# First halves one step sooner, and weight conversions dealt out: a fused gated-attention and SoLU kernel on Trainium2

## The chip, the cores and the metric

The kernel runs on one core of one Trainium2 chip. The metric is the device time of one execution in microseconds (us). Below, PE is TensorE, DVE is VectorE, ACT is ScalarE, POOL is GpSimd and SP is the engine whose queue issues most of the transfers.

## What is computed

Two blocks follow each other. The first is a gated linear attention over 4 batches, 8 heads, 768 tokens and a head size of 48, the second a feed-forward block over the 3072 tokens, with 384 inputs, 1024 hidden units and a layer norm between its two products. The reference, cut to its core:

```python
for t in range(S):
    state = alpha[:, :, t, :, None] * state + np.einsum('bhd,bhe->bhde', k[:, :, t], v[:, :, t])
    y[:, :, t] = np.einsum('bhd,bhde->bhe', q[:, :, t], state)
...
x = np.ascontiguousarray(attn_out.transpose(0, 2, 1, 3)).reshape(B * S, H * D)
...
h = x @ w_in
e = np.exp(h - h_max)
sm = e / (np.sum(e, axis=-1, keepdims=True) + 1e-09)
solu = h * sm
ln = (solu - mu) / np.sqrt(var + 1e-06) * g_ln
return (ln @ w_out).astype(np.float32)
```

The weights `w_in` and `w_out` arrive as 64-bit floats and are turned into 32-bit floats by integer and float operations on DVE.

## The kernel before

The 768 tokens are cut into 6 groups of 128. A group holds 4 batches, so the feed-forward works on 6 times 512 tokens, and its output on 24 chunks of 128 tokens, numbered n = 4 g + b. Period g is the time in which group g goes through the first product of the feed-forward, in 8 steps s (one for each 128 of the 1024 hidden units). In the same steps the attention of group g + 1 and the second product of group g - 1 are done. All of the order is written out by hand: each engine runs its instructions in the order of the program.

**A step.** `up(g, s)` is six PE instructions for h (`up_mm`; a product of 32-bit floats is two instructions in the trace), then ACT's exponential e, DVE's product u = h e and ACT's square of u (`up_act`). The banks for h are two, so the up of step s waits for the product of step s - 2. `running(g, s)` adds up e (on POOL) and the squares (on DVE) over the steps into p; in the last group DVE sums u too. At the next period's start `token_sums` takes p's sums over partitions (PE matmuls into `rows`, DVE's transpose into `cols`).

**The downs.** `down(n, half)` is the second product of chunk n for four of the eight hidden blocks: eight PE instructions into one of two banks `o`. The list `todo` holds the eight halves of one group, and each step of the next period takes one off its front. Behind a second half, the next step's up is followed by `finish(n)`: three small DVE instructions, a power on POOL (`r`), a scaled copy on ACT (`o_sb`), and an output transfer on SP. The last group's eight halves stand behind the last period, with its `token_sums` and `last_norm` behind the first of them.

**The attention.** The names in the tables `usual` and `first` place the parts of the next group's attention at the head of a step, behind the up, in the middle or at the tail: transposes and scans on DVE, `queries` and `keys` on POOL, `apart` and the copies of `keys_back` on ACT, `scores`, `read_state`, `read_values` and `next_state` on PE. `read_values` ends with four ACT copies that make the next group's x.

**Period 0.** It comes first and holds, beside group 0's ups, the conversion of the weights in 8 pieces: pieces 0 to 3 are `w_in`, 4 to 7 `w_out`. `fetch` brings the raw bits into one of six slots of `room`, `in_range` is two ACT instructions (and two short reads of an accumulator) that test a piece, `bits` is the conversion by five DVE instructions (L612, L615, L620, L623, L624), and `scaled` is the multiplication of two rows of blocks of `w_out` by the gain on ACT. Behind the loop over f stand, in this order, `bits(6)`, the transposes of k, the second `array_sums`, `down(0, 0)`, `bits(7)`, `token_sums(0)`, `alpha_T(1)`, `down(1, 0)`, the scans of group 1, and `mean`, which takes the mean of the weights over the hidden units (`mean(0)` is L645). Then come group 1's queries and scores (L278).

Of the kernel before, what the change touches and what calls it, by code (L numbers as in the profile page):

```python
# [11 lines left out]
U32 = mybir.dt.uint32  # L12
I32 = mybir.dt.int32
AF = mybir.ActivationFunctionType
ALU = mybir.AluOpType
# [17 lines left out]
def fast_path(ctx, tc, q, k, v, alpha, moe_w_in, moe_w_out, moe_g_ln, out):  # L33
# [13 lines left out]
    B, H, S, D = q.shape  # L47
    NTOK, DM = out.shape
    DFF = moe_w_in.shape[1]
    G = S // P  # L50
# [5 lines left out]
    FC = DFF // P  # L56
# [116 lines left out]
    def load_v(g):  # L173
        t = slice(g * P, (g + 1) * P)
        for b in range(B):
            nc.sync.dma_start(out=held(vn, b), in_=v[b, :, t, :].rearrange("h p d -> p h d"))
# [188 lines left out]
    def next_state(g):  # L365
        kv = banks("kv", [H, D], 2)
        for h in range(H):
            for c in range(2):
                for r in range(4):
                    b = 2 * (r // 2) + c  # L370
                    nc.tensor.matmul(
                        kv[c][quarter(r), h], lhsT=kg[:, b, h, E0 * (r % 2) : E0 * (r % 2) + E0],
                        rhs=vn[:, b, HW * h + E1 : HW * h + HW], start=True, stop=True,
                        tile_position=(0, 32 * r), skip_group_check=True,
                    )
        for c in range(2):
            s = held(state, c)
            if g == 0:
                nc.scalar.copy(out=s, in_=kv[c])
            else:  # L380
                nc.vector.tensor_tensor(out=s, in0=s, in1=kv[c], op=ALU.add)

    def u_of(g, f):
        return slots[((0, 5, 4), (1, 2, 3))[g % 2][f // 3]][:, T4 * (f % 3) : T4 * (f % 3) + T4]

    def up(g, f):
        up_mm(g, f)
        up_act(g, f)

    def up_mm(g, f):  # L390
        d = gr[g]
        h = ps_h.tile([P, T4], FP, tag="h", name="h")
        for a in range(KC):
            nc.tensor.matmul(  # L394
                h, lhsT=w_in[:, a, f * P : (f + 1) * P], rhs=d["x"][:, a].rearrange("p b t -> p (b t)"),
                start=(a == 0), stop=(a == KC - 1),
            )
        d["h"] = h

    def up_act(g, f, between=None):  # L400
        d = gr[g]
        h = d["h"]
        if g:
            e, u2 = (ring.tile([P, T4], FP, name=x) for x in ("e", "u2"))
        else:
            e, u2 = (sT[:, f % 4, 4 * i : 4 * i + 4].rearrange("p b t -> p (b t)") for i in range(2))
        u = u_of(g, f)
        nc.scalar.activation(out=e, in_=h, func=AF.Exp)  # L408
        nc.vector.tensor_tensor(out=u, in0=h, in1=e, op=ALU.mult)  # L409
        if between:  # L410
            between()
        nc.scalar.activation(out=u2, in_=u, func=AF.Square)  # L412
        d[f] = e, u2
# [16 lines left out]
    def array_sums(g, half):  # L430


        d = gr[g]
        if half == 0:
            d["q"] = [ps_a.tile([P, T4], FP, tag=f"a{i}", name=f"quarters{i}") for i in range(2)]
        for i in range(2):
            for f in range(4):
                r = quarter(f)
                nc.tensor.matmul(
                    d["q"][i][r], lhsT=ones[:, 0:32], rhs=d[4 * half + f][i], start=half == 0, stop=half == 1,  # L440
                    tile_position=(0, r.start), skip_group_check=True,
                )
        if half:
            d["p"] = one.tile([P, 2, T4], FP, name="p")
            for i in range(2):
                nc.scalar.copy(out=d["p"][:, i], in_=d["q"][i])
            d["unit"] = small_ones
# [108 lines left out]
    float64 = moe_w_in.dtype != FP  # L556
# [4 lines left out]
    def place(i):  # L561
        kind, f = pieces[i]
        return w_out[:, f : f + 2, 0:DM] if kind else w_in[:, :, f * P : f * P + 2 * P]
# [22 lines left out]
    made = {}  # L586
# [3 lines left out]
    def in_range(i, parts=(0, 1)):  # L590


        if not float64:
            return
        if 0 in parts:
            hi = raws[i][:, :, :, 1].bitcast(FP)
            squares[i] = one.tile([P, F], FP, name="sq").rearrange("p (c f) -> p c f", c=hi.shape[1])
            nc.scalar.activation(out=squares[i], in_=hi, func=AF.Square, accum_out=far[:, i, 0:1])
        if 1 in parts:
            sq = squares.pop(i)  # L600
            nc.scalar.activation(out=sq, in_=sq, func=AF.Exp, scale=-(2.0**24), accum_out=far[:, i, 1:2])

    def bits(i, part=None):
        if not float64:
            return
        lo, hi = raws[i][:, :, :, 0], raws[i][:, :, :, 1]
        if part != 1:
            made[i] = [
                lots[2 * (i % 2) + x].rearrange("p (c f) -> p c f", c=hi.shape[1]) for x in range(2)
            ]  # L610
            top = made[i][0].bitcast(U32)
            nc.vector.tensor_scalar(  # L612
                out=top, in0=hi, scalar1=3, scalar2=0x3FFFFFF8, op0=ALU.logical_shift_left, op1=ALU.bitwise_and
            )
            nc.vector.scalar_tensor_tensor(  # L615
                out=top, in0=hi, scalar=0xC0000000, in1=top, op0=ALU.bitwise_and, op1=ALU.bitwise_or
            )
        if part != 0:
            top, low = made.pop(i)
            nc.vector.tensor_scalar(  # L620
                out=low.bitcast(U32), in0=top.bitcast(U32), scalar1=0xFF800000, scalar2=None, op0=ALU.bitwise_and
            )
            nc.vector.scalar_tensor_tensor(out=low, in0=lo, scalar=2.0**-52, in1=low, op0=ALU.mult, op1=ALU.mult)  # L623
            nc.vector.tensor_tensor(out=place(i), in0=low, in1=top, op=ALU.add)  # L624

    def scaled(i):
# [77 lines left out]
    for i in range(3):  # L704
        part = slice(NP * i, NP * i + NP)
# [5 lines left out]
    for i in (0, 2, 1):  # L711
        if i == 1:
            scan_on(0, i)
        part = slice(NP * i, NP * i + NP)
        nc.vector.tensor_tensor(
            out=qe[:, :, 0:P] if i == 2 else qv[:, part, 0:P], in0=t[i], in1=aT[:, part, 1:SW], op=ALU.mult
# [13 lines left out]
    keys_back(0)  # L730
    in_range(0)
    bits(1)
    in_range(1)

    for f in range(FC):
        up_mm(0, f)
        if f == 4:
            array_sums(0, 0)
        up_act(0, f, (lambda: in_range(2 + f // 2, (f % 2,))) if f < 6 else None)

        bits(2 + f // 2, f % 2)
        if f == 0:
            next_state(0)
            fetch(4, 3)
            load_first(k, kn, 1)
            load_first(q, qn, 1)
            load(alpha, an, 1)
        elif f == 2:
            ends_k = ends_of(kn, "e")
        elif f == 3:  # L750
            fetch(5, 1)
            fetch(6, 2)
            ends_q = ends_of(qn, "u2")
        elif f == 5:
            fetch(7, 3)
            load_v(1)
        elif f == 6:
            scaled(4)
    bits(6)
    tk = three("tp_k", [(ps_a, "a2"), (ps_a, "a3"), (ps_h, "h")])  # L760
    turned(kn, ends_k, tk)
    load(k, kn, 2)
# [11 lines left out]
    for i in range(3):  # L774
        scan_back(1, i)
        part = slice(NP * i, NP * i + NP)
# [19 lines left out]
    for i in range(2):  # L796
        scan_on(1, i)
        part = slice(NP * i, NP * i + NP)
# [110 lines left out]
    todo = []  # L909
    for g in range(1, G + 1):  # L910
        rise, att = g < G, g + 1 < G
        plan = first if g == 1 else usual

        def at(where, s):
            for what in plan[where].get(s, "").split() if att else ():
                attend(g + 1, what)

        after = 3 if g == 1 else None
        if not rise:
            break  # L920
        for s in range(FC):
            at("head", s)
            if rise:
                up(g, s)
            if after is not None:
                finish(after)
                after = None
            if s == 0 and g < 3:
                next_state(g)
            if s == 0 and g > 1:  # L930
                token_sums(g - 1)
            at("behind", s)
            for f in centres.get(s, ()) if g == 1 else ():
                centre(f)
            if rise and s:
                running(g, s)
            at("middle", s)
            if todo:
                n, half = todo.pop(0)
                down(n, half)  # L940
                if half:
                    after = n
            at("tail", s)
        if after is not None:
            finish(after)
        todo = [(n, half) for n in range(g * B, g * B + B) for half in range(2)]


    for n, half in todo[:2]:
# [14 lines left out]
    def compare(out, x, bound, op):  # L964
# [6 lines left out]
        out=chunks[:, :, 2], in0=sums[:, :, 2], scalar=0.25, in1=sums[:, :, 3], op0=ALU.mult, op1=ALU.is_le  # L971
# [6 lines left out]
    else:  # L978
# [9 lines left out]
        out=bad, in0=all_ok[0:1, 0:1], scalar1=float(P * ends[-1]), scalar2=None, op0=ALU.is_lt  # L988
# [451 lines left out]
```

## Time and profile before

Three runs gave 374.48, 374.51 and 374.62 us.

| | |
|---|---|
| median of the runs | 374.51 us |
| the profiled execution: its own time | 374.51 us |
| its span in the profile | 372.6 us |
| mean granted TensorE clock | 0.995 |
| busy: PE, DVE, ACT, POOL | 361.1, 244.9, 147.2, 124.6 us |
| second product (L507), first product (L394), busy on PE | 134.8, 132.2 us |

Times in the views count from the span's start. A row of a timeline gives the start, the time to the end of the last instruction that is merged into it, the engine, the line, the operation, what is written and read, the number of instructions, and in brackets how long the engine was idle before it and what ended that. Matmuls overlap, so the time from one row's start to the next row's start says how long PE spent on a row. In the table by stretches, each row is a part of the span: its length, the busy time and instruction count of each engine, the granted clock (1.00 is full), and the share of the transfer engines.

### The profile page before, as it was taken

Reading aid. Unit: us, or ns where it says so; the run is one execution under the profiler, and the core shown is the slowest. Engines: PE = TensorE matmul, PEld = TensorE weight load, DVE = VectorE, ACT = ScalarE, POOL = GpSimd, SP = SyncE. Lnnn points to the kernel's source line nnn. Section 1 sums busy time; section 2 is a strip of 40 time slices with the busy share of each in tenths; the row PEclk is TensorE's granted clock in tenths of the full one; section 3 lists DMA queues with packets and bytes.
Section 4 is the critical chain, followed back from the end, with each engine's and each line's share of the span. In section 5 each row is a group of like instructions: output and inputs, shape, how many; then the busy total and the mean of one; then the engine's idle time right before and its main releaser. Section 6 shows DMA issues by size and latency. Waiting matters only on the chain. (4 is left out here: it accounts for less than half of the span.)

```text
span 372.6 us, 10040 instructions
## 1 busy us (share of the span) xinstructions
PE 361.1 (97%) x4341; PEld 215.8 (58%) x4341; DVE 244.9 (66%) x375; ACT 147.2 (40%) x260; POOL 124.6 (33%) x129
## 2 busy tenths in 40 slices
PE   8889999979999999999999999999999999999994
PEld 7775355556755566566575566575555565555552
DVE  1997979978998888945666945666946223544500
ACT  3649853591556262251532251532231231332100
POOL 7020000001367973573114573114582211333200
PEclk9999999998999999999999999999999999999999
DMA  9995986066177608453036253004050000000011
GB/s 181 187 326 144 217 270 139 2 135 152 67 161 165 153 3 168 111 137 84 25 86 145 68 136 86 25 4 106 21 129 9 23 23 0 24 22 21 30 39 49
DMA packets 72871, 36.06 MB, mean 97 GB/s; under 512 B 48232, under 2 KB 70000, under 8 KB 72816
## 3 DMA queue, kind: packets, MB, share of 16 engines
q1 hardware_dynamic: 71792, 34.39, 39.5%
q10 hardware_dynamic: 1024, 0.92, 0.7%
q8 instruction: 36, 0.59, 0.7%
q14 instruction: 19, 0.16, 0.1%
HBM read 25.30 MB, written 4.72 MB: 81 GB/s over the span
## 5 line engine op out<-in xcount | busy, mean ns | idle before, releaser
L507 PE MATMUL o<-w_out,room 128*128 128x385 f32 x384 | 134.8, 495 | 0.0
L394 PE MATMUL h<-x,w_in 128*128 128x512 f32 x288 | 132.2, 599 | 0.6 <-ACT x L363 0.6
L507 PEld LDWEIGHTS o<-w_out,room 128*128 128x128 f32 x384 | 71.6, 191 | 55.3 <-issue 14.7
L394 PEld LDWEIGHTS h<-x,w_in 128*128 128x128 f32 x288 | 52.7, 189 | 58.3 <-issue 48.4
L409 DVE TENSOR_TENSOR room<-h,e 128x512 f32<-128x512 f32 x40 | 27.6, 690 | 60.0 <-ACT e L408 60.0
L408 ACT ACTIVATE e<-h 128x512 f32<-128x512 f32 x40 | 23.9, 597 | 93.8 <-PE h L394 93.6
L427 POOL TENSOR_TENSOR p<-p,e 128x512 f32<-128x512 f32 x30 | 42.5, 1416 | 27.3 <-ACT e L408 27.0
L412 ACT ACTIVATE u<-room 128x512 f32<-128x512 f32 x40 | 25.2, 630 | 38.2 <-DVE room L409 38.2
L546 POOL TENSOR_TENSOR r<-sums,mhalf 128x1 f32<-128x1 f32 x20 | 12.8, 639 | 77.3 <-DVE sums L537 77.1
L289 DVE TENSOR_TENSOR sT<-a,mask 128x512 f32<-128x512 f32 x43 | 26.7, 683 | 14.4 <-PE a L278 14.4
L427 DVE TENSOR_TENSOR p<-p,u 128x512 f32<-128x512 f32 x30 | 24.4, 814 | 7.2 <-ACT u L412 7.2
L204 DVE TENSOR_TENSOR_SCAN hT<-aT,unit 128x516 f32<-128x516 f32 x18 | 23.4, 1342 | 7.6 <-ACT aT L697 7.5
L204 DVE TENSOR_TENSOR_SCAN aT<-aT,seed 128x516 f32<-128x516 f32 x18 | 27.9, 1578 | 0.2
L278 PEld LDWEIGHTS a<-qv,kT 32*128 32x128 f32 x704 | 21.9, 189 | 8.8 <-DVE qv L799 2.7
L278 PE MATMUL a<-qv,kT 32*128 32x128 f32 x704 | 24.6, 282 | 2.1 <-DVE qv L799 1.9
L333 PE MATMUL y<-sT,vn 128*32 128x128 f32 x768 | 22.9, 274 | 1.0 <-issue 0.8
L212 POOL COPY fend<-hT 128x12 f32<-128x12 f32 x6 | 4.1, 676 | 59.0 <-DVE hT L204 59.0
L333 PEld LDWEIGHTS y<-sT,vn 128*32 128x32 f32 x768 | 20.8, 110 | 4.4 <-issue 3.8
L225 POOL TENSOR_TENSOR kT<-kT,hT 128x1024 f32<-128x1024 f32 (+1 forms) x8 | 14.2, 1805 | 21.1 <-DVE kT L179 21.1
L196 ACT ACTIVATE sq<-an,mone 128x1536 uint8<-128x1536 f32 x12 | 18.9, 1575 | 0.2
L548 ACT ACTIVATE o_sb<-o,r 128x384 f32<-128x384 f32 x16 | 9.3, 581 | 24.1 <-POOL r L546 24.1
L363 ACT COPY x<-y 128x384 f32<-128x384 f32 x24 | 11.2, 479 | 7.3 <-PE y L333 7.1
(148 smaller groups left out, 364.5 us busy)
## 6 DMA issues: line engine op xcount, KB each, us to landing
vn<-in_v_dram SPq DMA_DIRECT2D x24, 192.0 KB, 4.4
an<-in_alpha_dram SPq DMA_DIRECT2D x20, 192.0 KB, 4.2
out_dram<-o_sb SPq DMA_DIRECT2D x20, 192.0 KB, 1.9
room<-in_moe_w_out_dram SPq DMA_DIRECT2D x8, 384.0 KB, 4.8
kn<-in_k_dram SPq DMA_DIRECT2D x16, 192.0 KB, 4.2
qn<-in_q_dram SPq DMA_DIRECT2D x16, 192.0 KB, 3.9
lot<-qe SPq DMA_DIRECT2D x40, 64.5 KB, 2.1
lot<-qv SPq DMA_DIRECT2D x20, 129.0 KB, 2.4
```

What stands on the lines that cost most here:

```text
L196: nc.scalar.activation(out=sq, in_=x, func=AF.Relu, scale=sign, bias=mone, accum_out=over[:, g, i : i + 1])
L204: nc.vector.tensor_tensor_scan(out=o, data0=a, data1=s, initial=1.0, op0=ALU.mult, op1=ALU.add)
L225: nc.gpsimd.tensor_tensor(out=kT[:, part], in0=kT[:, part], in1=hk[:, part], op=ALU.mult)
L278: nc.tensor.matmul(a[b][:, i], lhsT=kT[quarter(b), kb], rhs=qv[quarter(b), qb, 0:P], start=not last and not i, stop=bool(last), tile_posit ...
L289: nc.vector.tensor_tensor(out=sT[:, b, half * NP : half * NP + NP], in0=a[b], in1=mask[:, None, :].to_broadcast([P, NP, P]), op=ALU.mult,)
L333: nc.tensor.matmul(y_bank(b)[quarter(r), a], lhsT=lhsT, rhs=rhs, start=(b, r) not in begun, stop=stop, tile_position=(row, 32 * r), skip_g ...
L394: nc.tensor.matmul(h, lhsT=w_in[:, a, f * P : (f + 1) * P], rhs=d["x"][:, a].rearrange("p b t -> p (b t)"), start=(a == 0), stop=(a == KC ...
L408: nc.scalar.activation(out=e, in_=h, func=AF.Exp)
L409: nc.vector.tensor_tensor(out=u, in0=h, in1=e, op=ALU.mult)
L412: nc.scalar.activation(out=u2, in_=u, func=AF.Square)
L427: eng.tensor_tensor(out=p, in0=d[0][i] if f == 1 else p, in1=d[f][i], op=ALU.add)
L507: nc.tensor.matmul(d["o"][:, 0 : DM + 1], lhsT=u_of(g, f)[:, b * P : b * P + P], rhs=w_out[:, f], start=(f == 0), stop=(f == FC - 1), skip ...
```

## The change

It has two parts.

In period 0, `bits` is split into its five instructions (`bit(i, k)`), and the loop over f takes a stated number of them from one list for pieces 2 to 7 behind each up: 4, 2, 2, 2, 5, 2, 3 and 10. Before, each f had the first two or the last three instructions of a piece, for pieces 2 to 5. The call `bits(6)` behind the loop is taken out. The checks `in_range` are laid out by a table: piece 1's moves from ahead of the loop to f = 4, and both parts of piece 4's to f = 5.

In the periods 1 to 4, the first half of the period's own group is put into `todo` in step 7, where the list is empty by then, and so is that step's down (in period 1 the period's only one). The next period starts with the second half. Period 5 gets seven halves of group 4, and its last step has none; group 5's eight halves stay behind it.

```diff
-    def bits(i, part=None):
-        if not float64:
-            return
+    def bits(i, steps=range(5)):
+        for k in steps if float64 else ():
+            bit(i, k)
+
+    def bit(i, k):
         lo, hi = raws[i][:, :, :, 0], raws[i][:, :, :, 1]
...
     bits(1)
-    in_range(1)
+
+    steps = [(i, step) for i in range(2, 8) for step in range(5)]
+    checks = {0: [(2, 0)], 1: [(2, 1)], 2: [(3, 0)], 3: [(3, 1)], 4: [(1, 0), (1, 1)], 5: [(4, 0), (4, 1)]}
+
+    def check(f):
+        for i, part in checks.get(f, ()):
+            in_range(i, (part,))
 
     for f in range(FC):
         up_mm(0, f)
         if f == 4:
             array_sums(0, 0)
-        up_act(0, f, (lambda: in_range(2 + f // 2, (f % 2,))) if f < 6 else None)
-
-        bits(2 + f // 2, f % 2)
+        up_act(0, f, lambda: check(f))
+        for _ in range((4, 2, 2, 2, 5, 2, 3, 10)[f]):
+            step = steps.pop(0)
+            if float64:
+                bit(*step)
...
         elif f == 6:
             scaled(4)
-    bits(6)
     tk = three("tp_k", [(ps_a, "a2"), (ps_a, "a3"), (ps_h, "h")])
...
             at("middle", s)
+            if s == FC - 1 and g < G - 1:
+                todo.append((g * B, 0))
             if todo:
                 n, half = todo.pop(0)
                 down(n, half)
...
-        todo = [(n, half) for n in range(g * B, g * B + B) for half in range(2)]
+        todo = [(n, half) for n in range(g * B, g * B + B) for half in range(2)][g < G - 1 :]
```

More of the change, by code (lines that the diff above doesn't have):

```diff
@@ L601, in in_range @@
             nc.scalar.activation(out=sq, in_=sq, func=AF.Exp, scale=-(2.0**24), accum_out=far[:, i, 1:2])
-    def bits(i, part=None):
-        if not float64:
-            return
+    def bits(i, steps=range(5)):
+        for k in steps if float64 else ():
+            bit(i, k)
+    def bit(i, k):
         lo, hi = raws[i][:, :, :, 0], raws[i][:, :, :, 1]
-        if part != 1:
+        if k == 0:
             made[i] = [
@@ L610, in bits @@
             ]
-            top = made[i][0].bitcast(U32)
+        top, low = made[i]
+        bits_top = top.bitcast(U32)
+        if k == 0:
             nc.vector.tensor_scalar(
-                out=top, in0=hi, scalar1=3, scalar2=0x3FFFFFF8, op0=ALU.logical_shift_left, op1=ALU.bitwise_and
+                out=bits_top, in0=hi, scalar1=3, scalar2=0x3FFFFFF8, op0=ALU.logical_shift_left, op1=ALU.bitwise_and
             )
+        elif k == 1:
             nc.vector.scalar_tensor_tensor(
-                out=top, in0=hi, scalar=0xC0000000, in1=top, op0=ALU.bitwise_and, op1=ALU.bitwise_or
+                out=bits_top, in0=hi, scalar=0xC0000000, in1=bits_top, op0=ALU.bitwise_and, op1=ALU.bitwise_or
             )
-        if part != 0:
-            top, low = made.pop(i)
+        elif k == 2:
             nc.vector.tensor_scalar(
-                out=low.bitcast(U32), in0=top.bitcast(U32), scalar1=0xFF800000, scalar2=None, op0=ALU.bitwise_and
+                out=low.bitcast(U32), in0=bits_top, scalar1=0xFF800000, scalar2=None, op0=ALU.bitwise_and
             )
+        elif k == 3:
             nc.vector.scalar_tensor_tensor(out=low, in0=lo, scalar=2.0**-52, in1=low, op0=ALU.mult, op1=ALU.mult)
+        else:
             nc.vector.tensor_tensor(out=place(i), in0=low, in1=top, op=ALU.add)
```

## The prediction

> **What bounds the kernel now.** First the page: TensorE is busy for nearly the whole span, so a change pays only where PE stands idle, runs slowly, or gets more work.
>
> ```profile
> PE 361.1 (97%) x4341; PEld 215.8 (58%) x4341; DVE 244.9 (66%) x375; ACT 147.2 (40%) x260; POOL 124.6 (33%) x129
> ```
>
> Then the timeline of PE, for its gaps (last bracket: idle before the row and who ended it).
>
> ```profile
> 66.46 1.63 PE L645 MATMUL sums<-w_out,ones 128*32 128x384 f32 x16 [0.57 <-DVE cols L467]
> ...
> 79.77 0.48 PE L278 MATMUL a<-qv,kT 32*128 32x128 f32 x2 [0.54 <-DVE qv L799]
> 81.64 2.64 PE L278 MATMUL a<-qv,kT 32*128 32x128 f32 x62 [1.38 <-DVE qv L799]
> 84.21 3.91 PE L507 MATMUL o<-w_out,room 128*128 128x385 f32 x8
> ...
> 136.95 2.84 PE L394 MATMUL h<-x,w_in 128*128 128x512 f32 x6 [0.60 <-ACT x L363]
> ...
> 340.30 2.74 PE L394 MATMUL h<-x,w_in 128*128 128x512 f32 x6
> 342.87 5.35 PE L507 MATMUL o<-w_out,room 128*128 128x385 f32 x16
> 348.15 0.65 PE L462 MATMUL rows<-p,ones 128*32 128x64 f32 x32
> ```
>
> Behind 28 us PE waits for DVE before the weight mean (66.46) and before group 1's scores (79.77, 81.64), and for ACT's copies of x at the end of period 1 (136.95). From there to the end no gap is left. The down half at 84.21 takes 3.84 us to the next row, where others take 2.6 to 2.8. The table by stretches says why:
>
> ```profile
> core 0: us, PE busy (x) PEld busy (x) DVE busy (x) ACT busy (x) POOL busy (x), PEclk, DMA share, GB/s
> 65.88:69.29 3.41, 2.84 (x22) 1.41 (x21) 3.31 (x7) 1.61 (x3) 0.00 (x0) 1.00 0.00 0
> ...
> 79.53:82.95 3.42, 1.80 (x46) 1.61 (x50) 2.02 (x3) 3.33 (x8) 0.00 (x0) 1.00 0.67 131
> 82.95:86.36 3.41, 3.41 (x30) 2.27 (x24) 2.45 (x5) 2.04 (x6) 0.00 (x0) 0.50 0.55 122
> ```
>
> After the pause before the scores the granted clock is 0.50 for 3.41 us. That costs half of it, 1.71 us of PE work. Last, DVE's timeline:
>
> ```profile
> 34.27 0.69 DVE L409 TENSOR_TENSOR room<-h,sT 128x512 f32<-128x512 f32 x1 [1.88 <-ACT sT L408]
> ...
> 48.87 0.69 DVE L409 TENSOR_TENSOR room<-h,sT 128x512 f32<-128x512 f32 x1 [1.22 <-ACT sT L408]
> ...
> 54.81 0.69 DVE L409 TENSOR_TENSOR room<-h,sT 128x512 f32<-128x512 f32 x1 [0.74 <-ACT sT L408]
> ...
> 61.92 0.55 DVE L612 TENSOR_SCALAR lot<-room 128x768 uint32<-128x768 uint32 x1
> 62.51 0.96 DVE L615 SCALAR_TENSOR_TENSOR lot<-room,lot 128x768 uint32<-128x768 uint32 x1
> 63.50 0.56 DVE L620 TENSOR_SCALAR lot<-lot 128x768 uint32<-128x768 uint32 x1
> 64.10 0.96 DVE L623 SCALAR_TENSOR_TENSOR lot<-room,lot 128x768 f32<-128x768 uint32 x1
> 65.09 0.96 DVE L624 TENSOR_TENSOR w_out<-lot 128x768 f32<-128x768 f32 x1
> 65.97 0.44 DVE L467 STREAM_TRANSPOSE cols<-rows 128x256 f32<-128x256 f32 x1
> ```
>
> One piece's conversion is five instructions, 61.92 to 65.97: 4.05 us. From 54.81 to 81.58, where the second product of `qv` ends, DVE has no gap: up to the scores DVE is the bound.
>
> **Part 1, conversions.** The new counts 4+2+2+2+5+2+3+10 make 30 steps: pieces 2 to 7 in full. `bits(6)` behind the loop is deleted, but `bits(7)` behind `scaled(6)` stays: piece 7 is converted twice, five more DVE instructions, +4.05 us, in the stretch that DVE bounds. Against that stands the idle that dealing out recovers. `in_range(1)` leaves ACT's queue ahead of the first exponential: its 2.0 us there (31.72 to 33.66) ended DVE's 1.88 of waiting at 34.27. Later the load of q, copied by ACT at 44.16, holds the exponential of f=4 to 44.69 in both kernels, so DVE's product of f=4 starts at about 45.3 (45.50 now). From there it needs four products of 0.605 us (start to start) and, with the double, five pieces of 4.04: 45.31+2.42+20.2=67.93. Now the transpose of `cols` starts at 65.97. I find every later input ready: fetches of pieces 5 and 6 go out about 1 us earlier, piece 7's also, and the two checks put into f=4 and f=5 end before the squares are missed. So the chain is late by 67.93-65.97=1.96 us. Bounds: 0.20 if all 3.84 us of the three idles were won, 4.05 if none; I take the queue as worked out, because its only fixed input (44.16) is a row.
>
> What is late: `cols`, the weight mean, group 1's scans, the scores. PE stands from 65.6 to 68.4 instead of to 66.46, then is done with its own work at about 81.06 (79.08 now: 76.47 and a half of 2.6), and the second `qv` product ends at 83.54.
>
> **Part 2, the clock.** The three changes of the granted clock, at 4.44, 82.95 and 86.36, lie on one grid of 3.413 us. The pauses before the scores (79.08 to 79.78, 79.99 to 81.64) fall inside one stretch of it; moved by 1.96 they are split by 82.95, the first stretch keeping 1.5 us of dense downs. The new pause of 2.8 us lies in the stretch 65.88 to 69.29 and may cost half speed from 69.29 to 72.70; then PE gets to the scores at 82.8, still ahead of 83.54, and the pause there shrinks to 0.7. Either way the slow stretch no longer hits work that counts: -1.71 (bounds 0 and -1.71; the nearest row, 1.80 us busy of few-row matmuls, is poorer than what I expect in either stretch).
>
> The Trainium skill, "TensorE: Matmul & The Clock Gate", Part 1, has the clock halve after an idle window of about 3.4 us. This trace differs: it halved after a stretch with 1.80 us busy. By the rule no pause of 2.8 us would halve it either, and the sum would be the same as mine; by the row, read as "a pause of 2.4 us halves it wherever it lies", it would be 1.71 higher.
>
> With a DVE that comes back 2 us later than PE, DVE stays behind a little in period 1, where group 2's queries meet their scores closely (117.72): 0 to 0.6, I take 0.3.
>
> **Part 3, the downs.** Each first half moves one place up: period 1's last step gains one half, the steps of periods 2 to 4 keep one each, period 5's last step loses one; matmuls in all: the same. In period 1 the half stands after the values and covers the wait for x: +2.70 for it, -0.68 (the last gap of the values is 0.88 us there, 0.20 in periods 2 to 4), -0.10 for the up behind it: +1.92. Its inputs are there: POOL has centred its rows of `w_out` by 130.6, and `finish(3)` freed its bank in step 0. At the end, -2.59 (a half, start to start), but that half covered the token sums. They need POOL's sum of step 7, and now `finish(19)` stands in that step, ahead of it on POOL. Step 6 of the same period has just that order now:
>
> ```profile
> 339.82 0.93 POOL L546 TENSOR_TENSOR r<-sums,mhalf 128x1 f32<-128x1 f32 x1 [5.00 <-DVE sums L537]
> 340.72 1.35 POOL L427 TENSOR_TENSOR p<-p,e 128x512 f32<-128x512 f32 x1
> ```
>
> The up of step 6 starts at 335.13, the sum ends at 342.07: 6.94 later. The token sums stand now at 348.15-340.30=7.85 behind their up; in the new kernel they could at 5.26, and wait until 7.0. So the gain is 0.85, not 2.59 (bounds 0 and 2.59). Part 3 is +1.07.
>
> The finishes move from steps 2, 4, 6 and the next period's head to 1, 3, 5, 7. In step 3 ACT's output copy waits for `r`, which on POOL stands behind the queries and a sum (to 162.6): ACT gets to `apart` and the four copies of the transposed keys at 163.7 instead of 160.08 and is done at 166.5; the scores at 166.62 take those banks. Twice (periods 2 and 3), 0 to 0.3 each; I take 0.1 in all. In step 5 `decay` queues behind `r`, to 175.6; the read at 178.75 covers it. In step 7 the copies of x end about 0.7 late, at 191.5; the up at 194.41 covers that. SP only gains: its output transfers get out of the way of the v loads.
>
> **Sum.** 1.96-1.71+0.3+1.92-0.85+0.1=+1.72. The profiled run is 374.51 (span 372.6, 1.9 around it), equal to the median: 376.2 us.
>
> **Rivals.** (a) The clock halves all the same before the scores' work, the pause having only moved: +1.71, less the 0.3: 377.6. For it: the pause before the scores is as long as now. Against: the grid. (b) A second halving at the end: the new wait of 1.75 us beside thin matmuls, in a poor place on the grid: 376.2+1.7=377.9. It needs that wait and the thin token sums in one stretch; by my times (347.9 to 349.6, cut at 349.19) they are not. (c) Not slower: the double conversion nearly vanishes in DVE's idle time. With all 3.84 us won the chain is 0.20 late, and with the slow stretch gone the whole is 0.20-1.71+1.07=-0.44: 374.1. It decides from a lateness of 1.39 us downward (then +0.75 or less). For it: the idles sum to almost one conversion. Against: the q load's copy at 44.16 and that PE would then pause nearly as now.
>
> **Chances.** Forecast 0.57 (375.3 to 377.1), (a) 0.20, (b) 0.08, (c) 0.15. About 0.2% (0.75 us) is what can be told from no change. (c) lies mostly within it: faster 0.04, same 0.12, slower 0.84. The range 375.2 to 377.9 leaves out most of (c) and half of (b).
>
> **What would show it.** In the new profile: nine conversions where there were eight, the last two both of piece 7; `cols` at 67.9; PE's wait for it about 2.6 us; PEclk 1.0 from 82.95 to 86.36; no wait for x at the end of period 1; `rows` at the end waiting about 1.7 us for POOL's `p`. I am wrong if `cols` is before 67, if a slice shows half clock behind 83, or if the token sums at the end start without a wait.

## The result, and the profile after

The changed kernel takes 376.63 us (median of 20 runs, 375.3 to 378.04), the kernel before 372.82 us (median of 20 runs, 372.28 to 374.62). The ratio is 1.0082, with a 95% interval from 1.0066 to 1.0098: slower by 0.8%. The forecast was 376.2 us and a range from 375.2 to 377.9, so the time, the side and the range hold. But the distance is larger than the sum's 1.72 (3.81 between the medians, some 3.1 by the ratio), because the kernel before is often faster than its three runs showed. Its runs fall on two levels: of 90 runs in this and the comparisons below, 39 lie at a median of 372.69 and 51 at 374.38, with none between 373.22 and 373.86. The three first runs and the profile were all of the upper level; of the 20 here 11 are of the lower, so their median lies just in it. The changed kernel has two groups as well, less clearly apart, 7 runs at 375.60 and 13 at 376.71, and its profiled execution (375.56 us, span 373.8) is of the lower.

The granted clock of the runs tells what the levels are. One stretch of 3.41 us at half speed takes 0.0046 off the mean granted clock of a run, and the half speed behind PE's last matmul, which all profiles but two have inside their span, takes at most 0.004. Of the 70 runs of before whose clock is on record, the 28 of the lower level have 0.998 to 1.000, and 41 of the 42 of the upper 0.991 to 0.995 (the other, 373.90 us, has 0.998). So the upper level goes with a half-speed stretch and the lower without. Of the changed kernel's 20 runs, 17 have 0.993 to 0.995, the whole upper group among them, and three of the lower group 0.997.

On the page's first line PE has the same instructions and nearly the same busy time, and DVE has five instructions and 4.1 us more. (POOL's busy time has grown with the same count. All profiled versions with the moved downs have 130.7 to 132.2 us, those without 123.7 to 124.6, so it goes with them; spans on POOL are rough.)

```profile
PE 361.8 (97%) x4341; PEld 216.4 (58%) x4341; DVE 249.0 (67%) x380; ACT 146.3 (39%) x260; POOL 132.2 (35%) x129
```

The timeline of PE (start, time to the end of the last merged instruction, what is written and read, in brackets the idle time before the row and what ended it):

```profile
68.27 2.79 PE L651 MATMUL sums<-w_out,ones 128*32 128x384 f32 x16 [2.36 <-DVE cols L467]
...
82.43 0.48 PE L278 MATMUL a<-qv,kT 32*128 32x128 f32 x2
83.41 2.06 PE L278 MATMUL a<-qv,kT 32*128 32x128 f32 x62 [0.50 <-DVE qv L812]
85.40 2.86 PE L507 MATMUL o<-w_out,room 128*128 128x385 f32 x8
...
136.48 2.86 PE L507 MATMUL o<-w_out,room 128*128 128x385 f32 x8
139.18 2.74 PE L394 MATMUL h<-x,w_in 128*128 128x512 f32 x6
...
342.31 2.74 PE L394 MATMUL h<-x,w_in 128*128 128x512 f32 x6
344.88 2.75 PE L507 MATMUL o<-w_out,room 128*128 128x385 f32 x8
349.30 0.65 PE L462 MATMUL rows<-p,ones 128*32 128x64 f32 x32 [1.66 <-POOL p L427]
```

The wait before the weight mean has grown from 0.57 to 2.36 us, the two waits before the scores (0.54 and 1.38) have shrunk to one of 0.50, the moved half at 136.48 stands where the 0.60 of waiting for x was, and the token sums at the end wait 1.66 for POOL. The table by stretches (its last row is the window that was slow in before):

```profile
core 0: us, PE busy (x) PEld busy (x) DVE busy (x) ACT busy (x) POOL busy (x), PEclk, DMA share, GB/s
64.80:68.22 3.42, 1.11 (x43) 0.84 (x32) 3.31 (x5) 0.33 (x1) 0.00 (x0) 1.00 0.02 5
68.22:71.63 3.41, 3.36 (x17) 1.18 (x18) 3.31 (x6) 1.22 (x3) 0.00 (x0) 0.50 0.00 0
...
82.95:86.36 3.41, 2.95 (x65) 2.55 (x66) 1.44 (x3) 3.31 (x7) 0.00 (x0) 1.00 0.64 123
```

In this execution the half speed came behind the new pause, on the weight mean (68.22 to 71.63), and not on the scores. PE had slack there: it reached the scores at 82.43 and still waited 0.50 for DVE. DVE's timeline shows piece 7 converted twice, and POOL's the order at the end:

```profile
59.55 0.56 DVE L616 TENSOR_SCALAR lot<-room 128x768 uint32<-128x768 uint32 x1
...
62.73 0.96 DVE L630 TENSOR_TENSOR w_out<-lot 128x768 f32<-128x768 f32 x1
63.72 0.56 DVE L616 TENSOR_SCALAR lot<-room 128x768 uint32<-128x768 uint32 x1
...
66.89 0.96 DVE L630 TENSOR_TENSOR w_out<-lot 128x768 f32<-128x768 f32 x1
67.77 0.44 DVE L467 STREAM_TRANSPOSE cols<-rows 128x256 f32<-128x256 f32 x1
```

```profile
347.00 0.93 POOL L546 TENSOR_TENSOR r<-sums,mhalf 128x1 f32<-128x1 f32 x1 [5.01 <-DVE sums L537]
347.90 1.35 POOL L427 TENSOR_TENSOR p<-p,e 128x512 f32<-128x512 f32 x1
```

The two full runs of L616 to L630, from 59.55 and from 63.72, write the same piece of `w_out` from the same raw bits. They put `cols` at 67.77, where it was at 65.97.

### The profile page after: what moved, and what is told of

The parts are those of the page before. It is cut to its first block, busy times and chain, and to the rows that moved or that the text cites. A ratio compares the mean times of both kernels' runs of the same rounds, so it can differ in the third digit from the quotient of the medians.

```text
span 373.8 us, 10040 instructions
## 1 busy us (share of the span) xinstructions
PE 361.8 (97%) x4341; PEld 216.4 (58%) x4341; DVE 249.0 (67%) x380; ACT 146.3 (39%) x260; POOL 132.2 (35%) x129
## 5 line engine op out<-in xcount | busy, mean ns | idle before, releaser
L394 PE MATMUL h<-x,w_in 128*128 128x512 f32 x288 | 132.2, 599 | 0.4 <-DVE g_col L642 0.4
L427 POOL TENSOR_TENSOR p<-p,e 128x512 f32<-128x512 f32 x30 | 43.7, 1456 | 20.0 <-ACT e L408 19.9
L546 POOL TENSOR_TENSOR r<-sums,mhalf 128x1 f32<-128x1 f32 x20 | 14.8, 741 | 71.2 <-DVE sums L537 71.0
L204 DVE TENSOR_TENSOR_SCAN hT<-aT,unit 128x516 f32<-128x516 f32 x18 | 24.2, 1390 | 7.9 <-ACT aT L703 7.8
L427 DVE TENSOR_TENSOR p<-p,u 128x512 f32<-128x512 f32 x30 | 22.4, 746 | 5.2 <-ACT u L412 5.2
L212 POOL COPY fend<-hT 128x12 f32<-128x12 f32 x6 | 3.1, 508 | 60.8 <-DVE hT L204 60.8
L261 POOL TENSOR_TENSOR state<-state,lot 128x384 f32<-128x384 f32 x10 | 8.8, 903 | 13.9 <-DMA lot<-qv 13.9
```

Of the source, the lines that this page charges most:

```text
L204: nc.vector.tensor_tensor_scan(out=o, data0=a, data1=s, initial=1.0, op0=ALU.mult, op1=ALU.add)
L394: nc.tensor.matmul(h, lhsT=w_in[:, a, f * P : (f + 1) * P], rhs=d["x"][:, a].rearrange("p b t -> p (b t)"), start=(a == 0), stop=(a == KC ...
L427: eng.tensor_tensor(out=p, in0=d[0][i] if f == 1 else p, in1=d[f][i], op=ALU.add)
L546: nc.gpsimd.tensor_tensor(out=r, in0=s[:, 3:4], in1=mhalf, op=ALU.pow)
```

## The experiments

All times are medians; each ratio is to the kernel before in the same comparison, where its median was 374.0 to 374.1 us, most of its runs being of the upper level. "After" is the changed kernel, "before" the old one. Differences between versions of different comparisons are uncertain by some tenths of a us: the lower level of before itself lay at 372.59 to 372.83 in the four comparisons, the upper at 374.31 to 374.57.

**One conversion taken out of after.** The second conversion of piece 7 does no part of the result, so it can go.

```diff
     scaled(6)
-    bits(7)
```

> The changed kernel without the second conversion of piece 7 (the call of bits(7) behind scaled(6) is taken out). My theory, that the second conversion costs what DVE's chain before the scores is late: the transpose of cols starts about 4.05 us earlier than in the changed kernel, near 63.8; PE's pauses before the weight mean and the scores shrink to under 1 us together, no half-speed stretch follows, and the time falls by the 1.8 us lateness, a further 2.0 to 2.3 that DVE is then early against the kernel before, and the clock's share: 371.5 to 372 us in nearly all runs. Rival, that the downs carry the loss: no more than 0.5 us below the changed kernel, about 376.

Measured: 371.54 us (371.17 to 371.68), ratio 0.9938 [0.9915, 0.9962]. `cols` starts 4.06 us before after's:

```profile
63.71 0.44 DVE L467 STREAM_TRANSPOSE cols<-rows 128x256 f32<-128x256 f32 x1
```

If the double conversion vanished in DVE's idle time, as rival (c) has it, taking it out would leave the time where it was; it falls by 5.09 us. Without it the change is faster than before.

**Part 1 alone, with the double and without.** Both leave the downs as they were before: no `todo.append` in step 7, and all eight halves in the list. The second also leaves `bits(7)` out.

```diff
-            if s == FC - 1 and g < G - 1:
-                todo.append((g * B, 0))
...
-        todo = [(n, half) for n in range(g * B, g * B + B) for half in range(2)][g < G - 1 :]
+        todo = [(n, half) for n in range(g * B, g * B + B) for half in range(2)]
```

> The changed kernel with the downs as in the kernel before: conversions dealt out and piece 7 converted twice. My theory: cols near 67.8 as in the changed kernel, the pause before the mean 2.4 us, and 1.0 to 1.1 us less than the changed kernel: 375.5. Rival, that the downs are free or a gain: the same time as the changed kernel or more, 376.6.

> Conversions dealt out, each piece once, the downs as before: part 1 of the change without its second conversion of piece 7. My theory: cols near 63.8, the scores reached 2 us sooner, no half-speed stretch ahead of or behind the scores: 370.4 to 370.9 us, one level, the fastest of the four. Rival, that PE and not DVE sets the time up to the scores: 372.5, as the kernel before in its fast runs.

Measured: 375.86 us (11 runs from 374.59 to 376.55, one at 380.71), ratio 1.0049 [1.0032, 1.0067], with the double; 371.03 us (370.33 to 371.68), ratio 0.9929 [0.9906, 0.9953], with each piece once. The double costs 4.83 us. In the kernel with each piece once, the pauses are small:

```profile
65.51 1.47 PE L651 MATMUL sums<-w_out,ones 128*32 128x384 f32 x16
...
79.14 2.06 PE L278 MATMUL a<-qv,kT 32*128 32x128 f32 x62 [0.60 <-DVE qv L811]
```

Its profile has no half speed from 4.25 us to PE's last matmul, and its six runs have a granted clock of 0.997 to 0.999. In the profile of the kernel with the double, the pause before the mean is as in after, but the scores still meet a late `qv`, and the half speed:

```profile
68.45 1.63 PE L651 MATMUL sums<-w_out,ones 128*32 128x384 f32 x16 [2.35 <-DVE cols L467]
...
83.63 3.66 PE L278 MATMUL a<-qv,kT 32*128 32x128 f32 x62 [1.38 <-DVE qv L812]
```

```profile
66.55:69.96 3.41, 1.50 (x16) 0.54 (x16) 3.27 (x7) 1.12 (x2) 0.00 (x0) 1.00 0.00 0
69.96:73.38 3.42, 3.42 (x11) 1.82 (x10) 3.38 (x4) 0.97 (x2) 0.00 (x0) 1.00 0.00 0
80.20:83.62 3.42, 1.50 (x6) 0.56 (x4) 3.31 (x4) 3.36 (x7) 0.00 (x0) 1.00 0.84 171
83.62:87.03 3.41, 3.40 (x62) 3.40 (x62) 0.00 (x0) 3.32 (x8) 0.00 (x0) 0.50 0.38 86
```

The 62 score products took 3.66 us instead of 2.06. This is rival (a) as it was described: the pause has moved, and the slow stretch behind it has moved with it. It is the same code up to the scores as in after, whose profile shows the other outcome. What differs is where the stretches are cut: at 66.55, 80.20 and 83.62 here, at 64.80 and 68.22 there, and so, four stretches of 3.413 later, at 81.87. Here the pause before the mean is split by a cut, and there it lies almost whole in one stretch.

**Part 3 alone.** This is the kernel before with only the moved downs, part 3 of the prediction.

```diff
+            if s == FC - 1 and g < G - 1:
+                todo.append((g * B, 0))
...
-        todo = [(n, half) for n in range(g * B, g * B + B) for half in range(2)]
+        todo = [(n, half) for n in range(g * B, g * B + B) for half in range(2)][g < G - 1 :]
```

> The kernel before with the downs moved one step sooner, the conversions untouched. My theory: +1.92 at the end of period 1, -0.85 at the token sums of the last group, so 1.07 us above the kernel before in the same state of its clock: 373.9 in the median, with a wait of 1.7 us for POOL's p ahead of the last token sums. Rival, that covering the wait for x is a gain as it stands: 0.6 us below the kernel before, 372.2.

Measured: 374.37 us (373.4 to 375.44), ratio 1.0022 [1.0002, 1.0042]. Its runs lie on two levels, 373.50 and 375.25, that is 0.81 and 0.87 above the levels of before. The profiled run (373.49) is of the lower level. Up to the scores it has the code of before and PE waits there as in before (0.53 and 1.38), but the clock stays full and the 62 products take 2.06 us, not 2.64. The end looks as in after:

```profile
347.12 0.65 PE L462 MATMUL rows<-p,ones 128*32 128x64 f32 x32 [1.66 <-POOL p L427]
```

So the downs cost 0.8 us here. In the other kernels they cost 0.77 (after less its version with the downs as before) and 0.51 (the same two with each piece once, 371.54 less 371.03).

**The late finish put behind the last sum.** In the last step of the last period `finish(19)` stands behind `running`, so that POOL's sum goes ahead of its power.

```diff
+            late = g == G - 1 and s == FC - 1
-            if after is not None:
+            if after is not None and not late:
...
+            if late and after is not None:
+                finish(after)
+                after = None
```

> The changed kernel with finish(19), in the last step of the last period alone, put behind the running sums instead of ahead of them. My theory: POOL's last sum then starts as soon as its exponential is there and no longer waits for the power; the last token sums start about 0.9 us sooner (DVE's sum of the squares is then last, 6.1 us behind the start of the up), and the time is 0.9 us below the changed kernel. Rival, that the order does not matter, since DVE ends last: no change against the changed kernel.

Measured: 375.92 us (374.54 to 377.14), ratio 1.0047 [1.0026, 1.0069], 0.7 us below after. PE and POOL:

```profile
344.45 2.74 PE L394 MATMUL h<-x,w_in 128*128 128x512 f32 x6
...
350.59 0.65 PE L462 MATMUL rows<-p,ones 128*32 128x64 f32 x32 [0.82 <-DVE sums L532]
```

```profile
348.02 1.27 POOL L427 TENSOR_TENSOR p<-p,e 128x512 f32<-128x512 f32 x1 [3.89 <-ACT e L408]
```

The token sums start 350.59-344.45=6.14 us behind their up instead of 6.99. POOL's sum is done at 349.29; what comes last now is DVE's own sum, at 350.45. (The bracket names L532, the copy of `finish(19)` that now stands straight behind that sum on DVE.) The order on POOL cost 0.85; DVE sets the next bound, 0.82 behind PE. One of DVE's sums just before (L424) took 1.20 us here, where POOL's sum runs at the same time, and 0.69 in after, where POOL's sum comes later; part of what the new order wins may be lost there.

**The downs moved, with their half kept at the end.** If the cost of part 3 is the half that leaves the end, and the wait there, the cost must go when the last period leaves out its first step's down and not its last one's. This version of part 3 alone adds only that.

```diff
-            if todo:
+            if todo and (s or g < G - 1):
```

> The kernel before with the downs one step sooner, and period 5 leaving out its first step instead of its last; the conversions are untouched. Theory, that the loss of the moved downs lies in the uncovered token sums alone: 0.6 to 0.7 us below the kernel before at each of its levels, 372.1 and 373.6 us, so about 1.5 us below the version that leaves out the last step. Rival, that the loss comes from the finishes in other steps: no more than 0.3 us below that version.

Measured: 373.12 us (371.65 to 374.01), ratio 0.9979 [0.996, 0.9998]. The levels are 371.96 and 373.38, 1.5 and 1.9 below part 3 alone: about the wait of 1.66 at the end, now covered by the half. The move itself is then a gain of 0.7 to 1.0.

**Both repairs.** Each piece once, the downs moved, period 5 without its first step's down (the two diffs above on after).

> Each piece converted once, and the downs moved one step sooner, but period 5, which has one half fewer, leaves out its first step instead of its last, so the token sums of the last group are covered by two halves as in the kernel before. My theory: the gain of 0.6 us at the end of period 1 is kept and the wait at the end is gone: 0.6 us below the version with dealt conversions alone, about 370.4. Rival, that the step without a down makes period 5 wait elsewhere: 371 or more.

Measured: 369.9 us (369.55 to 370.08), ratio 0.9899 [0.9874, 0.9923]. It is faster than both kernels, and 1.1 us below the version with dealt conversions alone, where 0.6 was expected. The end of its timeline has no wait:

```profile
338.41 5.35 PE L507 MATMUL o<-w_out,room 128*128 128x385 f32 x16
343.69 0.65 PE L462 MATMUL rows<-p,ones 128*32 128x64 f32 x32
```

**The pause filled with work.** These three test whether the clock is what makes two levels. Small matmuls go to columns of a bank that hold no data, ahead of the work that PE waits for; they add PE work only in the pause. The first puts 10 ahead of group 1's scores in before, the second 11 ahead of the mean and 10 ahead of the scores in after. With their start flag the half sum that the bank already holds is lost, and the outputs of these two versions are not whole: chunk 2 (and chunk 1 in the second) lacks that part. The other instructions and their order are the same.

```diff
+    def filler(n, count):
+        o = st[n]["o"]
+        for _ in range(count):
+            nc.tensor.matmul(
+                o[:, 385:512], lhsT=ones, rhs=ones[:, 0:127], start=True, stop=True, skip_group_check=True
+            )
...
+    filler(2, 10)
     scores(1, 0)
```

> The kernel before with ten extra matmuls of ones into unused columns of a bank, issued by PE between down(2, 0) and group 1's scores, about 2.2 us of work in a pause of 2.35 us. They add work and nothing to the result. My theory, that the kernel before has two levels because the pause before the scores halves the clock in some executions and not in others: only the low level is left, 372.4 to 373.0 us in all runs, granted clock 1.0 from 80 to 90 us. Rival, that the two levels come from elsewhere (transfers, the start): both levels stay, 372.4 to 373.0 and 373.9 to 374.9, or 2 us are added.

> The changed kernel with eleven such matmuls in the pause before the weight mean (2.6 us) and ten before the scores. My theory: what the changed kernel has over 1.8 us (the chain's lateness) and 0.8 us (the downs) is the halved clock behind the pauses; with the pauses filled the time is 372.75+1.8+0.8=375.4 in nearly all runs and the granted clock stays 1.0 from 10 us on. Rival, that the clock does not matter here since PE waits for DVE anyway: the median stays near 376.6.

Measured for before: 374.5 us (373.96 to 376.84), ratio 1.0033 [1.0014, 1.0052], 1.5 us above the upper end of what the theory expected. The rival's "2 us are added" meets the number, but not for its reason: the clock is full from 80 to 90, and 11 of the 12 runs have a granted clock of 0.997 to 1.000. In the profiled run, the slowest (376.84, clock 0.992), PE stands still later, and a half-speed stretch follows at 143.70:

```profile
139.92 0.65 PE L462 MATMUL rows<-p,ones 128*32 128x64 f32 x32
...
142.44 4.30 PE L507 MATMUL o<-w_out,room 128*128 128x385 f32 x8 [1.86 <-issue]
```

The bracket names no releaser. Why 20 more PE instructions (a product of 32-bit floats is two) come with that stop was not found, and the run decides nothing on the two levels.

Measured for after: 375.56 us (375.29 to 376.08), ratio 1.0047 [1.0028, 1.0067]: 1.07 below after, one level, expected 375.4. The granted clock of all nine runs is 0.997 to 1.000, and the profile is at full clock around both places:

```profile
64.80:72.00 7.20, 7.20 (x86) 5.17 (x78) 6.99 (x11) 1.61 (x3) 0.00 (x0) 1.00 0.01 2
80.00:88.00 8.00, 8.00 (x96) 6.20 (x94) 5.93 (x9) 6.72 (x14) 0.00 (x0) 1.00 0.75 160
```

The run on before was made again with 8 matmuls that carry no start flag, which leaves the result whole.

```diff
-                o[:, 385:512], lhsT=ones, rhs=ones[:, 0:127], start=True, stop=True, skip_group_check=True
+                o[:, 385:512], lhsT=ones, rhs=ones[:, 0:127], start=False, stop=True, skip_group_check=True
...
-    filler(2, 10)
+    filler(2, 8)
```

> The kernel before with eight extra matmuls of ones ahead of group 1's scores, about 1.8 us of the 2.35 us that PE pauses there, added into unused columns without a start flag, so the result is whole. With ten of them PE then stood 1.9 us at the start of period 2 for nothing that the profile names, which hid the answer; with eight, the code of PE lies otherwise. Theory, that the two levels of the kernel before are the halved clock behind that pause: the low level alone, 372.4 to 373.1 us, and no half-speed stretch before the end of the work. Rival, that PE gives back in period 1 what it wins at the scores, because other engines bind there: 374 us or more again, with a wait in period 1 or 2.

Measured: 373.23 us (372.58 to 373.56), ratio 0.9983 [0.9969, 0.9998], just above what was expected. All 12 runs lie within 1 us, at a granted clock of 0.996 to 1.000, and none at the upper level of before. The stop at 142 is gone, and the stretch before the scores is busy and keeps the clock:

```profile
79.53:82.95 3.42, 3.21 (x57) 2.90 (x59) 2.11 (x3) 3.33 (x7) 0.00 (x0) 1.00 0.58 119
82.95:86.36 3.41, 3.41 (x38) 2.09 (x30) 2.72 (x5) 2.16 (x6) 0.00 (x0) 1.00 0.62 137
```

So the upper level of before is the half-speed stretch behind the pause before the scores: its distance, 1.69 us, is about half of 3.41, its runs have the lower granted clock, and it goes when the pause is filled. The filled version is 0.5 us above the lower level (373.23 against 372.69), probably the price of the extra matmuls.

## Why the prediction was right, and where it was wrong

From the lower level of before, 372.69, the medians divide the change into three: dealing out each piece once -1.66 (to 371.03), the second conversion +4.83 (to 375.86), the downs +0.77 (to 376.63). From the upper level the first is -3.35, since no run of that version has the slow stretch's 1.7 us (granted clock 0.997 to 0.999).

**The double conversion: right.** It is there, on DVE, and it decides the sign. The lateness of `cols` was predicted as 1.96 and is 1.80. The fixed input of the sum, f=4's product behind the copy of q, was put at 45.31 and came at 45.14:

```profile
45.14 0.69 DVE L409 TENSOR_TENSOR room<-h,sT 128x512 f32<-128x512 f32 x1 [0.94 <-ACT sT L408]
```

The sum had 22.62 us from there to `cols`, and the trace has 22.63. Rival (c), the double hidden in DVE's idle time, needed a lateness of 1.39 or less; the 1.80 rejects it, and so do the 5.09 and 4.83 us that the double costs. The step was still read one-sidedly: it netted the double against the idle that dealing out wins, and so did not say that the change without it would be a gain. In `cols` the double is 4.06 us, in the medians 0.8 to 1.0 more. The 12 runs of the two versions without it have a granted clock of 0.997 to 1.000, those with it mostly 0.993 to 0.995, and after with its pauses filled is 1.07 faster: the rest is likely the clock, halved behind the longer pauses that the double makes.

**The clock: wrong.** This is the step that failed: "Either way the slow stretch no longer hits work that counts: -1.71", argued by the grid of 3.413 us. The spacing of the grid holds in every trace, but its phase belongs to the execution, not to the kernel. The first change to full clock came at 4.44 us in the profile of before, at 6.78 in after's, and between 4.00 and 7.19 in the ten others; all later changes lie at whole multiples of 3.413 us from it. "By the grid" therefore used edges of one execution for another. In before, the slow stretch is present on the upper level only, so -1.71 is no term of all of its runs: it comes off 374.38, not off 372.69. In after it falls on the mean, where PE's slack covers it, as profiled and as the prediction had allowed, or on the scores, as rival (a) had it, or, by the granted clock of three runs, 0.997, on neither. That it falls on the scores in after's upper group is not shown by a profile of after itself; the profiles of the version with the downs as before and of the one with the late finish, with the same code up to there, show half speed from 83.62 and 83.40. Forecast and rival (a) are no alternatives but outcomes of one program. The signs named (full clock from 82.95 to 86.36, a short wait of 0.50 against 0.7) came true in the one profiled execution.

The Trainium skill, "TensorE: Matmul & The Clock Gate", Part 1, says that the window is free-running and that one kernel differs from run to run with its phase. These traces agree, with the start from 4.00 to 7.19 us; the prediction had weighed the page's idle rule only, and left this sentence unused.

**Why the time was still hit.** This was partly luck. The base, 374.51, was of the upper level, 1.8 above the other, and from it the sum took off a slow stretch of 1.71. The two nearly cancel, and 376.2 is the lower level of before plus 3.5. From low to low level the distance is only 2.9 (372.69 to 375.60), as the lateness, the lag and the downs came out 0.16, 0.3 and some 0.2 smaller than in the sum. What the upper group of after has over that, 1.1 us (376.71), is likely a half-speed stretch on the scores, which the sum had excluded; with 13 of 20 runs it lifts the median above the forecast. The two profiles, upper to low, are 1.05 us apart (374.51 to 375.56), and 1.71 more for the slow stretch would make it 2.8.

**Period 1.** The lag was taken as 0.3 behind a net of 0.25, 0.55 together. The last `y` product before the end of period 1 came 0.21 late (132.64 to 132.85): the lag is not seen. The half at its end was right in the term: +1.92: the next row of PE, the products for the state (L371), starts 2.12 later, of which 0.21 is older. In before and in after:

```profile
139.72 1.57 PE L371 MATMUL kv<-vn,kg 128*32 128x48 f32 x128
```

```profile
141.84 1.57 PE L371 MATMUL kv<-vn,kg 128*32 128x48 f32 x128
```

**The downs.** The sum had +1.92-0.85=1.07, and the experiment on them alone 0.81 and 0.87. Missing is a gain that was not counted: at period 2's start PE gets from the products for the state to the token sums in 1.39 us (141.84 to 143.23) instead of 1.54 (139.72 to 141.26). In before DVE's p was done only at 141.11, in after at 141.46, so it is likely that the token sums no longer wait for it. The end is as worked out, 0.86 gained and 1.66 of waiting (0.85 and about 1.7 predicted), and its reason is shown by the finish behind the sum: POOL's order made 0.85 of it, DVE's sum the rest. The copies in step 3 cost nothing, where 0.1 was taken: from the down to the scores PE takes 2.69 us in both profiles (163.93 to 166.62, 165.88 to 168.57). Some 0.04 went instead at a read of the state in period 3, which took 1.14 us to the next row instead of 1.10; why is open. Rival (b), a second halving at the end, did not come: the clock was full there in the profile.

## What to carry to other kernels

When a list that deals out work replaces calls, count the pieces it covers against the calls that are left: the double here was worth 4.8 us, more than all that dealing out had won. A clock edge seen in one profile is a place that may move in the next run (by up to 3.2 us between the profiles here); price a half-speed stretch as a chance for each pause, not as a place, and ask of a few identical times whether they are all of one level. When a half leaves the end of a kernel for a fuller place, look at what it covered: leaving out the one at the start of the last period instead was 1.5 to 1.9 us better.

## What the runs showed of the hardware

The phase of the clock's windows differs from run to run, and through it one kernel has two times 1.69 us apart with no work changed. One run of before (373.90 us at 0.998) does not fit this, nor do two of the versions with moved downs (375.30 at 0.999, 373.22 at 0.997); they stay open. What in a stretch decides is not settled. Stretches of 3.41 us in which PE was busy 1.11 us (after, 64.80), 1.50 us (the dealt-out double, 80.20) and 1.80 us (before, 79.53) were each followed by half speed, though none of them was idle throughout; another with 1.50 us (the dealt-out double, 66.55) was not, nor was one with 2.03 us in before with the downs moved and the half kept at the end:

```profile
80.18:83.59 3.41, 2.03 (x63) 1.87 (x62) 1.41 (x3) 3.31 (x7) 0.00 (x0) 1.00 0.57 124
83.59:87.00 3.41, 3.41 (x32) 2.01 (x32) 3.41 (x5) 1.46 (x4) 0.00 (x0) 1.00 0.64 138
```

Busy time alone does not tell them apart. The stop of 1.86 us on PE that came with 20 more instructions and not with 16 stays open too.
